# Decode attention with a channel MLP: w2's last rows as 68 rows with four zeroed copies, and x's rows spread over 64 partitions

## The chip, the cores and the metric

The kernel runs on one core of one Trainium2 chip. The metric is the device time of one execution in microseconds, the median of several runs. Everything on VectorE (DVE), ScalarE (ACT), GpSimd (POOL), TensorE (PE) and SyncE (SP) is ordered by semaphores that the kernel sets itself.

## The reference

One decode step for 8 sequences (B = 8, one token each, D = 640) with 32 heads of 128 and a cache of 4096 keys, plus an MLP with F = 1728, all in bf16:

```
xn  = layernorm(x)
q   = xn @ wq                                  # (8, 32 heads, 128)
p   = softmax(q k^T / sqrt(128))               # 4096 keys per head and sequence
att = (p v) @ wo
y   = layernorm(xn)
mlp = gelu(y @ w1 + b1) @ w2 + b2
out = x + att + mlp
```

The two caches are 268 MB each; all else together is under 16 MB.

## The kernel before

**Tiles.** The work goes in NQ = 32 items: item i is one sequence and a group of 8 heads. Its keys fill 128 partitions x 32768 elements, 64 KB in each partition: a k tile and a v tile of 8.4 MB. SBUF holds three such slots, `S_sb[:, 0..2]`: k tiles alternate between slots KA and KB, every v tile goes to slot VS. The slots also hold the small data while they are free: `wq_sb` lies in VS before v tile 0; `x_sb`, `xn_sb`, `y_sb` and the norm's numbers lie in KB before k tile 1; w1 and w2 come into KA after the last k tile there. `w2b_sb` (w2's last rows) and `ones_sb` have a place of their own.

**Order.** Nothing is scheduled by a planner. Each step is entered with `at(position, function)`, the steps are sorted by position, and each adds its instructions to the list of its engine; the lists are then replayed. Within an engine the order is that of the positions. `wait` puts a semaphore wait ahead of the next instruction of an engine, and everything behind it on that engine waits too.

**Start.** SP issues wq, k tile 0, then (after the q matmuls, `tk["qmm"]`) k tile 1 and v tile 0. ACT issues x, b2 and w2b. GpSimd makes iotas and constants (`consts_pool`). DVE makes the identity and masks (`idents`), then the layernorm (`norm(0)`, `norm(1)`); PE transposes the result (`pe_xT`), DVE copies it to `xT_sb` (`cp_xT`), PE starts the output accumulator with x and b2 (`pe_acc0`) and, once wq is there, makes q (`pe_q`), which DVE copies to `qT_sb` (`cp_q`).

**An item.** GpSimd writes the item's q into `qrep_sb` (`qrep`); PE and ACT turn it into `qbc_sb`, q on every partition (`pe_qbc`, `act_qbc`). DVE takes 176 of the 256 keys of a partition in three chunks: multiply by q, add halves, reduce (`dve_chunk`). The other 80 are transposed by PE, evicted by ACT (`act_T`) and multiplied by PE (`pe_QK`); DVE picks them (`dve_sel`), finds the maximum (`dve_max`), ACT makes the exponentials (`act_exp`), PE multiplies with v (`pe_PV`). GpSimd normalizes (`o_norm`). `k_ready` is a GpSimd memset of one column behind a wait for the k tile, which PE's transposes wait for. GpSimd's order begins with the constants, then qrep(0), k_ready(0), qrep(1), and so on.

**Releases.** SP issues k tile i when DVE and PE have finished tile i - 2 (`tk[("km", i - 2)]`, `tk[("kt", i - 2)]`), and v tile i when PE has finished v tile i - 1:

```
            if i >= 2:
                sp.wait(tk[("kt", i - 2)], tk[("km", i - 2)])
            elif s == KB:
                sp.wait(tk["qmm"])
```

**MLP.** F = 13 x 128 + 64: 13 blocks of 128 rows (FB) and a last one of FLAST = 64 rows, whose rows of w2 are `w2b_sb`. `pe_mlp1`, `act_gelu` and `pe_mlp2` run while the last item's k tile is being worked on.

Of the kernel before, what the change touches and what calls it, by code (L numbers as in the profile page):

```python
# [9 lines left out]
F32 = mybir.dt.float32  # L10
# [4 lines left out]
P = 128  # L15
# [177 lines left out]
def bass_parallel_sum__gqa_block_cached__mixer_channel_mlp__decode_kernel(  # L193
# [13 lines left out]
    B, _, D = A_x.shape  # L207
    _, H, SK, DH = A_k_cache.shape
    F = B_w1.shape[1]
# [5 lines left out]
    NQ = NHQ * B  # L215
    DC = D // P
    FB = F // P
    FLAST = F - FB * P
    SCALE = float(DH) ** -0.5
    TPB = 8  # L220
    NS = 2
# [5 lines left out]
    RW = P // HW  # L227
    NL = 3
    WN_CUT = (0, 5, 7, HS)
    V_CUT = (0, 192, 256)  # L230

    def jp_of(i):
# [14 lines left out]
    x2 = A_x.rearrange("b s d -> (b s) d")  # L247
    out2 = out.rearrange("b s (c n) -> (b s c) n", n=P)

    with ExitStack() as es:  # L250
# [7 lines left out]
        def part(slot, lo, n, rows=P):  # L258
            return S_sb[0:rows, slot, lo:lo + n]
# [3 lines left out]
        def scratch(n, rows=P, slot=KB):  # L263
            ap = part(slot, o_[slot], n, rows)
            o_[slot] += n + n % 2
            return ap
# [8 lines left out]
        woW_sb = part(KB, 0, HW * D)  # L275
        woL_sb = part(KB, HW * D, 2 * HS * D).rearrange("p (g x) -> p g x", g=2)
        b2_sb = scratch(D, 1)
        x_sb = scratch(D, B)
        xn_sb = scratch(D, B)
        y_sb = scratch(D, B)  # L280
        st_sb = scratch(64, B).bitcast(F32).rearrange("p (w n) -> p w n", w=2)
        iota_i = scratch(2 * P).bitcast(I32)
        iota_h = scratch(2 * HS).bitcast(I32)
        mtmp = scratch(2 * 2 * HS).bitcast(F32).rearrange("p (w n) -> p w n", w=2)
# [5 lines left out]
        ones_sb = sb("ones_sb", [1, B], BF)  # L290
        w2b_sb = sb("w2b_sb", [FLAST, D], BF)
        xT_sb = sb("xT_sb", [P, 2, DC, B], BF)
# [11 lines left out]
        ident_bf = sb("ident_bf", [P, P], BF)  # L304
# [16 lines left out]
        TR_ps = ps("TR_ps", [P, 2, TPB * P], BF)  # L321
# [4 lines left out]
        ACC_ps = ps("ACC_ps", [P, 512], F32)  # L326
# [8 lines left out]
        pe, dve, act, sp, pool = (_Eng(sem(f"{n}_s")) for n in ("pe", "dve", "act", "sp", "pool"))  # L335
        pe2, act2 = _Eng(sem("pe2_s")), _Eng(sem("act2_s"))
        ld_s = [_Dma(sem(f"ld_s{s}")) for s in range(3)]
        ld_x, ld_b1, ld_b2, ld_wq, ld_w1, ld_w2a, ld_w2b, st_o = (
            _Dma(sem(n)) for n in ("ld_x", "ld_b1", "ld_b2", "ld_wq", "ld_w1", "ld_w2a", "ld_w2b", "st_o"))
        ld_vl = [_Dma(sem(f"ld_vl{q}")) for q in range(1, len(V_CUT) - 1)]  # L340
        ld_wl = [_Dma(sem(f"ld_wl{q}")) for q in range(2)]
        ld_wn = [_Dma(sem(f"ld_wn{q}")) for q in range(len(WN_CUT) - 1)]
        tk = {}
        prog = []

        def at(pos, fn, *a):
            prog.append((pos, len(prog), fn, a))

        def load(key, dma, dst, src, eng=None):
            tk[key] = dma.sig((eng or sp).dma_start(dst, src))  # L350
# [18 lines left out]
        def load_v(i):  # L369
# [4 lines left out]
            tk[("v", i)] = []  # L374
            for d, lo, hi in zip([ld_s[VS]] + ld_vl, V_CUT[:-1], V_CUT[1:]):
                if lo:
# [15 lines left out]
        def load_wn(q):  # L392
            lo, hi = WN_CUT[q], WN_CUT[q + 1]
            n = HS * DH
            tk[("wn", q)] = ld_wn[q].sig(sp.dma_start(
                woL_sb[:, 1, lo * D:hi * D],
                A_wo[NL * n:(NL + 1) * n, :].rearrange("(p s) n -> p (s n)", p=P)[:, lo * D:hi * D]))

        def consts_pool():
            pool.iota(iota_h, [[-HP, HS]], base=0, channel_multiplier=1)  # L400
            pool.iota(iota_w, [[-RW, HW]], base=0, channel_multiplier=1)
            tk["iota"] = pool.sig(pool.iota(iota_i, [[1, P]], base=0, channel_multiplier=-1))
            for d, (ap, v) in zip([None] + ld_vl + [None] * 2, (
                    (zeros_sb, 0.0), (ones_sb[:, :], 1.0), (mx_sb[:, :], 0.0), (mb_sb[:, :], 0.0))):
                inst = pool.memset(ap, v)
                if d is not None:
                    inst.call[3] = (d.sem, 1)
            tk["consts"] = pool.sig(pool.memset(ones_f[:, :], 1.0))
# [45 lines left out]
        def pe_xT(w):  # L454
            src = xn_sb if w == 0 else y_sb
            pe.wait(tk["xn" if w == 0 else "y"], tk["id"])
            TRB[w].use(pe)
            for c in range(DC):
                last = pe.transpose(TR_ps[:, w, c * B:(c + 1) * B], src[:, c:D:DC], ident_bf[0:B, 0:B])
            TRB[w].used(pe, pe.sig(last))  # L460

        def cp_xT(w):
            TRB[w].use(dve)
            tk[("xT", w)] = TRB[w].used(dve, dve.sig(dve.tensor_copy(
                xT_sb[:, w, :, :].rearrange("p c b -> p (c b)"), TR_ps[:, w, 0:DC * B])))

        def pe_q():
            pe.wait(tk["wq"], tk[("xT", 0)])
# [12 lines left out]
        def pe_acc0():  # L481
            pe.wait(tk["consts"], tk["x"], tk["b2"], tk["id"])
            pe.matmul(ACC_ps[:, 0:DC * B], zeros_sb, zeros_sb[:, 0:DC * B], start=True, stop=False,
                      skip_group_check=True)
            for c in range(DC):
                pe.matmul(ACC_ps[:, c * B:(c + 1) * B], x_sb[:, c * P:(c + 1) * P], ident_bf[0:B, 0:B],
                          start=False, stop=False, skip_group_check=True)
                pe.matmul(ACC_ps[:, c * B:(c + 1) * B], b2_sb[:, c * P:(c + 1) * P], ones_sb[:, :],
                          start=False, stop=False, skip_group_check=True)

        def fcols(c):
            return (slice(c, FB * P, FB), P) if c < FB else (slice(FB * P, F), FLAST)

        def pe_mlp1():
            pe.wait(tk["w1"], tk["b1"], tk[("xT", 1)])
            TRB[1].use(pe)
            for c in range(FB + 1):
                cols, rows = fcols(c)
                o = HT_ps[0:rows, c * B:(c + 1) * B]
                for kc in range(DC):  # L500
                    pe.matmul(o, w1_sb[:, kc, cols], xT_sb[:, 1, kc, :], start=(kc == 0), stop=False)
                last = pe.matmul(o, b1_sb[:, cols], ones_sb[:, :], start=False, stop=True)
            TRB[1].used(pe, pe.sig(last))

        def act_gelu():
            TRB[1].use(act)
            act.activation(hT_sb[:, 0:FB, :].rearrange("p c b -> p (c b)"), HT_ps[:, 0:FB * B],
                           ACT.Gelu_apprx_tanh)
            tk["h"] = TRB[1].used(act, act.sig(act.activation(
                hT_sb[0:FLAST, FB, :], HT_ps[0:FLAST, FB * B:(FB + 1) * B], ACT.Gelu_apprx_tanh)))  # L510

        def pe_mlp2():
            pe.wait(tk["h"], tk["w2a"], tk["w2b"])
            for fc in range(FB + 1):
                rows = P if fc < FB else FLAST
                w = w2_sb[:, fc, :] if fc < FB else w2b_sb
                for c in range(DC):
                    last = pe.matmul(ACC_ps[:, c * B:(c + 1) * B], w[:, c * P:(c + 1) * P],
                                     hT_sb[0:rows, fc, :], start=False, stop=False, skip_group_check=True)
            tk["mlp"] = ACCB.used(pe, pe.sig(last))  # L520
# [132 lines left out]
        def pe_PV(i):  # L653
            PVB.use(pe)
            pe.wait(tk[("exp", i)])
            for j in range(NKEY):
                if j == 0:
                    pe.wait(tk[("v", i)][0])
                elif j in V_CUT:
                    pe.wait_ge(ld_vl[V_CUT.index(j) - 1].sem, 1)  # L660
                last = pe.matmul(PV_ps[:, 0:HS], tile[VS][:, j, :], P_sb[:, :, j],
# [89 lines left out]
        def fin_wn(q):  # L751
            lo, hi = WN_CUT[q], WN_CUT[q + 1]
            pe.wait(tk[("wn", q)], tk[("oS", 3, 0)], tk[("oS", 3, 1)])
            for r in range(lo, hi):
                for c in range(DC):
                    last = pe.matmul(ACC_ps[:, c * B:(c + 1) * B],
                                     woL_sb[:, 1, r * D + c * P:r * D + (c + 1) * P], oS3_sb[:, r, :],
                                     start=False, stop=(r == HS - 1), skip_group_check=True)
            if hi == HS:
                ACCB.used(pe, pe.sig(last))  # L760
# [12 lines left out]


        Q = 100.0
        at(-900, load, "x", ld_x, x_sb, x2, act)
        at(-898, load, "b2", ld_b2, b2_sb, B_b2.rearrange("(o f) -> o f", o=1), act)
        at(-890, load, "wq", ld_wq, wq_sb, A_wq.rearrange("(p c) n -> p c n", c=DC))
        at(NQ * Q - 55, load_mlp)
        at(-897, load, "w2b", ld_w2b, w2b_sb[:, :], B_w2[FB * P:F, :], act)  # L780
        at(-870, load_k, 0)
        at(-800, consts_pool)
        at(-795, idents)
        at(NQ * Q - 60, sel_pool)
        at(-790, norm, 0)
        at(-780, pe_xT, 0)
        at(-776, maskw)
        at(-775, cp_xT, 0)
# [7 lines left out]
        at(NQ * Q - 11.5, pe_mlp1)  # L796
        at(NQ * Q - 11, act_gelu)
        at(NQ * Q + 4.6, pe_mlp2)
        for i in range(NQ):
            o = i * Q  # L800
            last = i == NQ - 1
# [8 lines left out]
            w = 42.0 / nt  # L810
# [20 lines left out]
        o = NQ * Q  # L831
        for q in range(2):
            at(o + 50 + 0.1 * q, load_wl, q)
            at(o + 79.1 + 0.2 * q, fin_wl, q)
        for q in range(len(WN_CUT) - 1):
            at(o + 51 + q, load_wn, q)
# [71 lines left out]
```

## Time and profile before

| | before |
|---|---|
| median of 3 runs | 1282.38 us (1282.24 to 1282.55) |
| profiled execution | 1282.34 us |
| its span | 1281.0 us |
| DVE busy | 1103.0 us, 86% |
| PE busy | 672.2 us, 52% |
| ACT busy | 476.1 us, 37% |
| POOL busy | 100.0 us, 8% |
| bytes moved | 551.99 MB at 431 GB/s over the span |
| mean granted TensorE clock | 0.557 |

Times on the page are microseconds from the span's start. Nearly all instructions carry line 111, the line that replays the lists, so groups are told apart by the names out<-in. A line of the timeline gives start, duration, engine, operation with shape, and in brackets the idle time before it and what ended that. "SPq" and "ACTq" lines are DMA issues of SP and ACT. q1 is SP's DMA queue, q10 is ACT's; each runs on the core's 16 DMA engines. Packet records, one for each packet with its queue, start, duration and size, are part of the trace; where a text says "packet records", numbers come from these.

### The profile page before, as it was taken

What the parts mean: (1) busy time and instruction counts of PE and PEld (TensorE: products, weight loads), DVE (VectorE), ACT (ScalarE), POOL (GpSimd) and SP (SyncE); (2) the same over time, 40 slices, a digit from 0 to 9 for tenths busy, and PEclk for the clock granted to TensorE, in tenths of its full rate; (3) what the DMA queues carried; (4) which work ended last, traced back from release to release, by engine and by line L of the source; (5) the groups of instructions that cost most, each with busy time, mean ns of one, the idle gap of its engine ahead of it and who ended that gap; (6) DMA issues with size and microseconds to landing.
All of it is one profiled execution on the core that took longest, in us unless ns stands there. A gap on an engine that the chain in (4) does not pass through costs nothing.

```text
span 1281.0 us, 34439 instructions
## 1 busy us (share of the span) xinstructions
PE 672.2 (52%) x13944; PEld 575.5 (45%) x13944; DVE 1103.0 (86%) x680; ACT 476.1 (37%) x905; POOL 100.0 (8%) x110
## 2 busy tenths in 40 slices
PE   1546555446545446555456554456454466464476
PEld 1435445345534345444345444345343355353365
DVE  1899999889888899888898888898888898888895
ACT  0524444233444233443234443234443234442331
POOL 0000010000000000000000000000000000000040
PEclk9755565555555555555565565555555565555565
DMA  9999999999999999999999999999999999999998
GB/s 400 445 422 436 432 432 434 434 436 432 432 432 440 428 432 436 440 426 432 438 438 428 430 436 442 428 430 436 440 430 428 436 436 436 426 438 432 432 439 361
DMA packets 10675, 551.99 MB, mean 431 GB/s; under 512 B 1244, under 2 KB 1445, under 8 KB 1702
## 3 DMA queue, kind: packets, MB, share of 16 engines
q1 hardware_dynamic: 10512, 551.70, 99.7%
q8 instruction: 9, 0.15, 0.0%
q10 hardware_dynamic: 150, 0.11, 0.0%
q14 instruction: 4, 0.03, 0.0%
HBM read 551.80 MB, written 0.01 MB: 431 GB/s over the span
## 4 chain that ended last, share of the span: by engine, by line
DMA 52%; DVE 36%; issue 11%; DVEq 0%; PE 0%; SPq 0%; ACT 0%
DMA S_sb<-in_A_k_cache_dram 51%; DVE S_sb L111 26%; DVE Sd_sb L111 8%; DMA S_sb<-in_A_wo_dram 2%; DVE S_ps L111 1%; DVE ri_sb L111 0%; DVEq L109 0%; PE ACC_ps L111 0%; DVE mx_sb L111 0%; SPq L111 0%; DVE mbT_sb L111 0%; DVE mxT_sb L111 0%; DVE mq_sb L111 0%; DVE mb_sb L111 0%; PE QB_ps L111 0%
## 5 line engine op out<-in xcount | busy, mean ns | idle before, releaser
L111 PE MATMUL TR_ps<-ident_bf,S_sb 128*128 128x128 bf16 (+1 forms) x2570 | 342.9, 280 | 353.5 <-POOL kr_sb L111 341.6
L111 DVE TENSOR_TENSOR S_sb<-S_sb,qbc_sb 128x7552 bf16<-128x7552 bf16 (+1 forms) x96 | 392.6, 4089 | 128.4 <-DMA S_sb<-in_A_k_cache_dram 128.1
L111 PEld LDWEIGHTS TR_ps<-ident_bf,S_sb 128*128 (+2 forms) x2570 | 245.4, 103 | 411.6 <-issue 337.7
L111 DVE TENSOR_REDUCE Sd_sb<-S_sb 128x59 f32<-128x3776 bf16 (+1 forms) x96 | 390.2, 4064 | 6.0
L111 ACT ACTIVATE KT_sb<-TR_ps 128x1024 bf16<-128x1024 bf16 x320 | 326.5, 1023 | 122.0 <-PE TR_ps L111 110.9
L111 PE MATMUL PV_ps<-P_sb,S_sb 128*128 128x8 bf16 x8192 | 224.0, 175 | 137.4 <-DMA S_sb<-in_A_v_cache_dram 134.5
L111 PEld LDWEIGHTS PV_ps<-P_sb,S_sb 128*128 128x128 bf16 x8192 | 221.5, 103 | 140.1 <-DMA S_sb<-in_A_v_cache_dram 137.3
L111 DVE TENSOR_TENSOR S_sb<-S_sb 128x3776 bf16<-128x3776 bf16 (+1 forms) x96 | 204.6, 2131 | 3.3
L111 ACT ACTIVATE P_sb<-Sd_sb,NB_sb 128x256 bf16<-128x256 f32 x256 | 126.3, 494 | 213.4 <-DVE NB_sb L111 213.4
L111 PE MATMUL S_ps<-qrep_sb,KT_sb 128*128 128x8 bf16 x2560 | 121.9, 177 | 51.6 <-ACT KT_sb L111 48.4
L111 ACT ACTIVATE oU_sb<-PV_ps 128x8 f32<-128x8 f32 x31 | 5.5, 177 | 375.6 <-PE PV_ps L111 375.6
L111 PEld LDWEIGHTS S_ps<-qrep_sb,KT_sb 128*128 128x128 bf16 x2560 | 91.8, 103 | 83.0 <-ACT KT_sb L111 42.1
L111 POOL TENSOR_TENSOR oT_sb<-oU_sb,ri_sb 128x8 bf16<-128x8 f32 x31 | 71.8, 2315 | 378.8 <-DVE S_sb L111 303.2
L111 POOL COPY qrep_sb<-qT_sb 128x128 bf16<-128x128 bf16 x32 | 14.5, 453 | 475.3 <-PE S_ps L111 455.2
L111 ACT ACTIVATION_READ_ACCUMULATOR P_sb<-Sd_sb,NB_sb 128x1 f32 x256 | 47.8, 187 | 0.0
L111 DVE TENSOR_TENSOR S_ps<-S_ps,mask_sb 128x320 f32<-128x320 f32 (+1 forms) x65 | 31.6, 486 | 2.6 <-PE S_ps L111 2.6
L111 DVE TENSOR_REDUCE Sd_sb<-S_ps 128x40 f32<-128x320 f32 x64 | 31.5, 491 | 2.2
L111 PE MATMUL QB_ps<-ident_bf,qrep_sb 128*128 128x128 bf16 x32 | 9.1, 284 | 41.2 <-DVE S_sb L111 21.4
L111 ACT ACTIVATE qbc_sb<-QB_ps 128x128 bf16<-128x128 f32 x32 | 8.9, 277 | 58.0 <-PE QB_ps L111 58.0
L111 POOL MEMSET kr_sb<- 128x1 f32 x32 | 3.1, 98 | 294.7 <-DMA S_sb<-in_A_k_cache_dram 294.7
L111 PEld LDWEIGHTS QB_ps<-ident_bf,qrep_sb 128*128 128x128 bf16 x32 | 3.3, 103 | 44.1 <-ACT oU_sb L111 29.5
L111 PE MATMUL CH_ps<-rs_sb,ones_f 128*128 128x8 f32 x64 | 16.5, 330 | 6.6 <-ACT P_sb L111 6.6
(71 smaller groups left out, 147.0 us busy)
## 6 DMA issues: line engine op xcount, KB each, us to landing
S_sb<-in_A_v_cache_dram SPq DMA_DIRECT2D x1, 6144.0 KB, 26.8
S_sb<-in_A_wq_dram SPq DMA_DIRECT2D x1, 5120.0 KB, 16.0
S_sb<-in_A_wo_dram SPq DMA_DIRECT2D x1, 2560.0 KB, 16.5
S_sb<-in_B_w_dram SPq DMA_DIRECT2D x1, 2160.0 KB, 30.3
S_sb<-in_B_w_dram SPq DMA_DIRECT2D x1, 2080.0 KB, 34.8
S_sb<-in_A_v_cache_dram SPq DMA_DIRECT2D x1, 2048.0 KB, 31.3
S_sb<-in_A_wo_dram SPq DMA_DIRECT2D x1, 1280.0 KB, 19.3
S_sb<-in_A_wo_dram SPq DMA_DIRECT2D x1, 800.0 KB, 20.8
```

The source lines that it names most:

```text
L111: inst = getattr(e, name)(*a, **k)
```

## The change

Two parts. First, w2's last block becomes FLAST = 68 rows: the last 64 rows of F and the four before them, which block structure also computes in the 13 full blocks. The four doubled rows of `w2b_sb` are set to zero by GpSimd after the load (`zero_w2b`), and `pe_mlp2` waits for that. The new step stands in GpSimd's order behind the constants and ahead of qrep(0). As 68 rows the load runs on four DMA engines; as 64 it ran on 16.

Second, x's eight rows go to partitions 0, 8, ..., 56 of a 64-partition `x_sb`, which GpSimd sets to zero first (`zero_x`, ahead of its constants); ACT's x load waits for that (`load_x`). The layernorms run on 64 partitions, the transposes give 64 columns of which `cp_xT` takes every eighth, and `pe_acc0` takes every eighth column of the identity.

```diff
-    FLAST = F - FB * P
+    FREST = F - FB * P
+    FLAST = FREST + 4
...
+    XP = 8 * B
...
-        x_sb = scratch(D, B)
-        xn_sb = scratch(D, B)
-        y_sb = scratch(D, B)
-        st_sb = scratch(64, B).bitcast(F32).rearrange("p (w n) -> p w n", w=2)
+        x_sb = scratch(D, XP)
+        xn_sb = scratch(D, XP)
+        y_sb = scratch(D, XP)
+        st_sb = scratch(64, XP).bitcast(F32).rearrange("p (w n) -> p w n", w=2)
...
+        def zero_x():
+            tk["xz"] = pool.sig(pool.memset(x_sb, 0.0))
+
+        def load_x():
+            act.wait(tk["xz"])
+            load("x", ld_x, x_sb[0:XP:8, :], x2, act)
...
-                last = pe.transpose(TR_ps[:, w, c * B:(c + 1) * B], src[:, c:D:DC], ident_bf[0:B, 0:B])
+                last = pe.transpose(TR_ps[:, w, c * XP:(c + 1) * XP], src[:, c:D:DC],
+                                    ident_bf[0:XP, 0:XP])
...
-                xT_sb[:, w, :, :].rearrange("p c b -> p (c b)"), TR_ps[:, w, 0:DC * B])))
+                xT_sb[:, w, :, :], TR_ps[:, w, 0:DC * XP].rearrange("p (c b o) -> p c b o", c=DC, o=8)[:, :, :, 0])))
...
-                pe.matmul(ACC_ps[:, c * B:(c + 1) * B], x_sb[:, c * P:(c + 1) * P], ident_bf[0:B, 0:B],
+                pe.matmul(ACC_ps[:, c * B:(c + 1) * B], x_sb[:, c * P:(c + 1) * P], ident_bf[0:XP, 0:XP:8],
...
-            return (slice(c, FB * P, FB), P) if c < FB else (slice(FB * P, F), FLAST)
+            return (slice(c, FB * P, FB), P) if c < FB else (slice(F - FLAST, F), FLAST)
...
+        def zero_w2b():
+            pool.wait(tk["w2b"])
+            tk["w2z"] = pool.sig(pool.memset(w2b_sb[0:FLAST - FREST, :], 0.0))
...
-            pe.wait(tk["h"], tk["w2a"], tk["w2b"])
+            pe.wait(tk["h"], tk["w2a"], tk["w2z"])
...
-        at(-900, load, "x", ld_x, x_sb, x2, act)
+        at(-905, zero_x)
+        at(-900, load_x)
...
-        at(-897, load, "w2b", ld_w2b, w2b_sb[:, :], B_w2[FB * P:F, :], act)
+        at(-897, load, "w2b", ld_w2b, w2b_sb[:, :], B_w2[F - FLAST:F, :], act)
...
         at(-800, consts_pool)
+        at(-799, zero_w2b)
         at(-795, idents)
```

## The prediction

> **What bounds the kernel now.** I read the page's slices and queues first. The profiled execution took 1282.34 us: a span of 1281.0 and 1.34 around it. The median of the three runs, 1282.38, is the same within 0.04, so what I add to the span I add to the median.
>
> ```profile
> DMA  9999999999999999999999999999999999999998
> q1 hardware_dynamic: 10512, 551.70, 99.7%
> q10 hardware_dynamic: 150, 0.11, 0.0%
> ```
>
> q1 is SP's queue (k, v and the big weights), q10 is ACT's (x, b2, w2b, b1, out). The 16 DMA engines are full from start to end on q1, so every microsecond in which SP has nothing queued moves the end, and compute costs only where it starves the queue. By the packet records no engine stands empty between 2 us and the tail. So the question is which buffer release comes too late. The timeline of the first 75 us has the releases:
>
> ```profile
> 0.74 0.60 ACTq L111 DMA_DIRECT2D S_sb<-in_A_x_dram  x1
> ...
> 1.63 0.53 ACTq L111 DMA_DIRECT2D w2b_sb<-in_B_w_dram  x1
> ...
> 16.82 4.43 PE L111 MATMUL CH_ps<-xT_sb,S_sb 128*128 128x8 bf16 x160 [8.00 <-DMA S_sb<-in_A_wq_dram]
> ...
> 21.77 0.29 POOL L111 COPY qrep_sb<-qT_sb 128x128 bf16<-128x128 bf16 x1 [20.06 <-DVE qT_sb L111]
> ...
> 22.44 0.28 ACT L111 ACTIVATE qbc_sb<-QB_ps 128x128 bf16<-128x128 f32 x1 [15.19 <-PE QB_ps L111]
> 36.46 4.03 DVE L111 TENSOR_TENSOR S_sb<-S_sb,qbc_sb 128x7424 bf16<-128x7424 bf16 x1 [14.75 <-DMA S_sb<-in_A_k_cache_dram]
> ```
>
> The query copy for tile 0 (qrep, GpSimd) is done at 22.06, the broadcast at 22.72; VectorE then sits until k tile 0 lands. That 13.7 us of slack belongs to GpSimd's step. SP's own timeline gives what hangs on VectorE:
>
> ```profile
> 21.64 0.43 SPq L111 DMA_DIRECT2D S_sb<-in_A_v_cache_dram  x1
> 69.25 0.33 SPq L111 DMA_DIRECT2D S_sb<-in_A_k_cache_dram  x1
> 85.34 0.33 SPq L111 DMA_DIRECT2D S_sb<-in_A_v_cache_dram  x1
> 103.58 0.33 SPq L111 DMA_DIRECT2D S_sb<-in_A_k_cache_dram  x1
> 128.85 0.33 SPq L111 DMA_DIRECT2D S_sb<-in_A_v_cache_dram  x1
> ```
>
> These are v0, k2, v1, k3, v2. k2 is issued when VectorE has finished tile 0 (69.25 = 36.46 + 32.79). The engines finish v0 at 73.05 to 74.90 (packet records). An issue takes 1.0 us to its first packet (wq: issued 0.74, first packets 1.77), so k2 comes 4.65 us before the last engine runs dry. That is the margin I test the change against: **VectorE may start tile 0 at most 4.65 us later, by 41.1.**
>
> **The change, part by part.**
>
> *x.* A GpSimd memset of 64x640 bf16 now precedes ACT's x load. Rows: 128x128 bf16 0.20 us, 128x128 f32 0.24; by bytes (256 B 0.20, 512 B 0.24, here 1280 B) 0.36, by elements five times 0.20, 1.0. The load leaves at 1.1 to 1.8 instead of 0.74. Queued behind it on ACT's queue are b2 and w2b; on GpSimd the iotas. More matters that x now arrives after wq's packets. Before, x's rows were first on eight engines and landed by 3.0; b2, issued at 1.37, had its one row served at 5.8, after two wq packets. I put x's rows there too, its completion one wq packet (1.57) later, and x on VectorE at 7.5 to 9 instead of 3.03. From 3.03 to PE's last ACC_ps matmul at 8.8 is 5.8 us, so all of it ends by 15, ahead of 16.8 when wq lets PE start. Were it not hidden, q would be late against the 13.7 us of slack. Norms on 64 partitions cost VectorE the same (its width, 640, stays), transposes 64 columns wide instead of 8 some tens of ns. Sum: 0, and nothing beyond 16.8 would show it.
>
> *w2b.* Before: 64 rows over 16 engines, four each, 14.3 us to land. How ACT's rows share an engine with SP's is in the DMA counts of the stretch 6.8 to 8.3 us:
>
> ```profile
> q1 hardware_dynamic: 15, 0.61, 96.9%
> q10 hardware_dynamic: 15, 0.02, 3.2%
> ```
>
> One small packet for one big one: a 1280 B row, 55 ns itself, waits out a 40 KB packet of wq, 1.51 to 1.65 us. The packet records say the same of one engine: b2's row at 5.8, b2's completion at 7.35, then four w2b rows, the completion at 15.4, each one wq packet after the one before; a 4-byte completion takes a turn of its own. On four engines each gets 17 rows, and the turns now last longer, since k tile 0 follows wq with 64 KB packets of 2.42 us.
>
> Count on the first engine: x row, x completion, b2 row, b2 completion, 17 rows, completion = 22 turns of q10, the n-th after q1's item n+1. Item 23 of q1: 8 wq packets and a completion, 8 of k0 and a completion, then the fifth packet of k1. k0 starts there at 15.4; 13 x (2.42 + 0.06) = 32.2, so w2b completes at 47.6, on GpSimd 0.5 later (k0: last completion 35.99, VectorE 36.46).
>
> By the Trainium skill, DMA: Bandwidth & Descriptors, section "Why a DMA increments its semaphore by 16 and not by 1", the engines are the largest number up to 16 that divides both sides' slowest dimension, which gives 4 for 68 rows. The trace agrees for 64 rows (16 completions) and x's 8 (8); no run here shows 68. Without that rule I have the title's "four", and the rows' ends: 16 engines (five rows each, landed near 17.5, cost 0) and one (b2: all 73 turns, done when v0 drains at 75, VectorE 40 late).
>
> *zero_w2b.* The new memset waits for w2b, and behind it in GpSimd's order stand qrep(0), k_ready(0) and all the rest; PE waits for qrep(0) with tile 0's transposes, ACT with the broadcast, VectorE with its first product. Price: 48.1, memset of 4x640 0.36 to 1.0 (0.5 taken, close to the byte rule), and 0.95 from qrep's start to the broadcast's end: VectorE starts at 49.6. **D = 49.6 - 36.46 = 13.2 us.** Less 4.65 of margin: the engines run dry from 74.9 until 69.25 + 13.2 + 1.0 = 83.5, **8.6 us**.
>
> *What is late next.* v2 waits for PE's tile 1, which hangs on ACT's exp(1) after VectorE's tile 1: 128.85 + 13.2 + 1.0 = 143.05, while k3, 133.16 before, now ends at 133.16 + 8.6 = 141.76: another **1.3 us**. v1 and k3 keep a margin: k3's issue 103.58 + 13.2 = 116.8 against v1's end 113.8 + 8.6 = 122.4. Later VectorE needs 34.5 us for a tile against 38.7 for the two transfers, gains 4.2 a tile and opens no further gap. The tail follows the transfers.
>
> *The last block with 68 rows* (PE, Gelu): same instruction counts, PE reads 68 weight columns instead of 64; 0, under 0.1 us. It sits before the last v lands.
>
> Sum: 8.6 + 1.3 = 9.9. The restart itself could add 0.5: wq's first packets took 1.9 to 2.7 us against 1.51. **1282.38 + 9.9 = 1292.3.**
>
> **The rivals.**
>
> *Nothing is starved (not slower).* An engine takes several q10 rows in one turn. Place: engines 0 to 3 between 5 and 47 us; it decides if w2b completes before 39.1 (41.1 less 0.5, 0.5 and 0.95), that is if the 22 turns shrink to 18. With all rows in one or two turns w2b lands before 15, GpSimd's memset ends long before 21.77, and what is left is x's rows no longer ahead of wq: the engine that began wq last, at 2.67, begins near 1.8. Time 1281.5 to 1282.4. For it: nothing here shows turns against 64 KB packets. Against it: 1:1 in the counts above, for four turns running on every engine. The Trainium skill, the same page, section "Queues, rings and completion order", says an engine drains a whole packet, typically 9 to 17 descriptors, from one ring before it switches; by that this rival would hold, and the trace's one row a turn speaks against it. Chance 0.07.
>
> *The 68 rows don't go to four engines* but to 16, as the 64 did: landed near 17.5, no cost, 1282.4. Chance 0.03; one or two engines (some 36 us more), 0.02.
>
> *Turns counted wrong.* If x still gets ahead of wq, or some completions take no turn, w2b is one or two turns of 2.48 earlier: D 10.7 or 8.2, time 1289.8 or 1287.3 (total D - 3.3). If q1's completions take no turn, two later: D 18.2, 1297.3. Same mechanism, other size. Chance 0.13 earlier, 0.07 later.
>
> *Faster.* Only x's place in the queue (0.9 us) and four rows fewer on 12 engines (0.23) gain: 1281.2 at best, no difference that can be measured. Chance of more 0.03, for a stagger of the engines (1.3 to 1.9 us in each landing) that I may misread.
>
> **How the numbers follow.** My count 0.65, the rest as above. About 0.2%, 2.6 us, can be told from no change. The low end, 1285, takes in the two turns fewer and a bubble shorter than counted; the high end, 1297, one turn more, the restart and a slow memset. Outside are the two uncosted cases (0.10), the faster one (0.03) and part of the later ones. Slower 0.65 + 0.13 + 0.07 + 0.02 = 0.87; same 0.10; faster 0.03.
>
> **What would show it.** w2b's issue to landing near 46 us instead of 14.3. GpSimd idle until 48, its reason w2b, then qrep. VectorE's first 128x7424 product at 49.6, k2's issue at 82.5, engines empty from 74.9 to 83.5, v2's issue near 142. x lands at 7.5 to 9, PE still starts on wq at 16.8. The forecast is wrong if w2b lands before 39, or if k2 is issued before 74 all the same.

## The result and the profile after

The changed kernel takes 1295.5 us, median of 5 runs (1295.26 to 1298.42), against 1282.38 us: 13.1 us more. The ratio on record is 1.0106 (95% interval 1.0092 to 1.0121; the two medians alone give 1.0102). The forecast was 1292.3 in a range of 1285.0 to 1297.0. The profiled execution took 1296.06 us with a span of 1294.7, 13.7 us longer than before's.

The profile's slices and queues, as shown of before:

```profile
DMA  9969999999999999999999999999999999999998
q1 hardware_dynamic: 10512, 551.70, 98.8%
q10 hardware_dynamic: 142, 0.11, 0.0%
```

The same bytes, but the third slice (64.7 to 97.1 us) is no longer full. The timeline of the first 52 us, the lines that answer to those of before:

```profile
1.39 1.16 ACTq L111 DMA_DIRECT2D S_sb<-in_A_x_dram  x1
...
2.90 0.26 ACTq L111 DMA_DIRECT2D w2b_sb<-in_B_w_dram  x1
...
9.21 0.88 DVE L111 BATCH_NORM_STATS2 S_sb<-S_sb 64x6 f32<-64x320 bf16 x2 [6.49 <-DMA S_sb<-in_A_x_dram]
...
16.17 4.43 PE L111 MATMUL CH_ps<-xT_sb,S_sb 128*128 128x8 bf16 x160
20.64 0.42 DVE L111 CAST qT_sb<-CH_ps 128x256 bf16<-128x256 f32 x1 [5.64 <-PE CH_ps L111]
...
48.67 0.63 POOL L111 MEMSET w2b_sb<- 4x640 bf16 x1 [46.39 <-DMA w2b_sb<-in_B_w_dram]
49.24 0.28 POOL L111 COPY qrep_sb<-qT_sb 128x128 bf16<-128x128 bf16 x1
...
49.90 0.28 ACT L111 ACTIVATE qbc_sb<-QB_ps 128x128 bf16<-128x128 f32 x1 [36.32 <-PE QB_ps L111]
50.29 4.02 DVE L111 TENSOR_TENSOR S_sb<-S_sb,qbc_sb 128x7424 bf16<-128x7424 bf16 x1 [29.23 <-ACT qbc_sb L111]
```

q is ready at 21.06, 0.6 us earlier than before, but GpSimd, idle for 46.39 us, waits for w2b until 48.67. VectorE's first product, which before waited for k tile 0, now waits for the broadcast of q and starts 13.83 us later. SP's timeline gives what hangs on it:

```profile
21.00 0.43 SPq L111 DMA_DIRECT2D S_sb<-in_A_v_cache_dram  x1
83.08 0.33 SPq L111 DMA_DIRECT2D S_sb<-in_A_k_cache_dram  x1
99.17 0.33 SPq L111 DMA_DIRECT2D S_sb<-in_A_v_cache_dram  x1
117.31 0.33 SPq L111 DMA_DIRECT2D S_sb<-in_A_k_cache_dram  x1
142.63 0.33 SPq L111 DMA_DIRECT2D S_sb<-in_A_v_cache_dram  x1
```

k2 is issued 13.83 us later than before and v2 13.78. The windows view of the stretch around it, after (columns: stretch, its length, busy us of PE, PEld, DVE, ACT and POOL with instruction counts, granted clock, DMA share, GB/s):

```profile
73.00:76.00 3.00, 2.98 (x45) 2.46 (x44) 3.00 (x1) 2.37 (x3) 0.00 (x0) 0.50 0.00 0
76.00:84.00 8.00, 6.50 (x87) 4.91 (x85) 7.79 (x7) 5.83 (x6) 0.29 (x1) 0.50 0.01 3
84.00:88.00 4.00, 0.00 (x0) 0.00 (x0) 3.93 (x4) 3.33 (x13) 0.00 (x0) 0.50 1.37 524
...
142.00:148.00 6.00, 3.02 (x40) 2.26 (x36) 5.93 (x3) 0.46 (x2) 2.65 (x2) 0.50 0.98 350
148.00:240.00 92.00, 51.16 (x986) 42.98 (x985) 87.66 (x52) 43.30 (x82) 5.82 (x7) 0.56 1.00 433
```

(A packet counts in the stretch in which it starts.) From 75.0, where the last engine ends v0, to 84.0 no big packet starts. A second, partial gap shows at 143: 350 GB/s instead of the 433 of the stretch beyond. The packet records put the last engine's completions behind those of before by 0.1 us at v0, 11.5 at k2 (105.80 against 94.28), 11.3 at v1 and at k3, 13.9 at v2 (166.41 against 152.50), and 13.7 to 13.9 from there to the end. All of the loss is made before 167 us, in two places.

### The profile page after: what moved, and what is told of

It is laid out like the page before. It is cut to its first block, busy times and chain, and to the rows that moved or that the text cites. A ratio compares the mean times of both kernels' runs of the same rounds, so it can differ in the third digit from the quotient of the medians.

```text
span 1294.7 us, 34441 instructions
## 1 busy us (share of the span) xinstructions
PE 673.5 (52%) x13944; PEld 576.7 (45%) x13944; DVE 1102.9 (85%) x680; ACT 476.8 (37%) x905; POOL 101.2 (8%) x112
## 4 chain that ended last, share of the span: by engine, by line
DMA 52%; DVE 35%; issue 11%; PE 1%; DVEq 0%; POOL 0%; SPq 0%; ACT 0%; ACTq 0%; POOLq 0%
DMA S_sb<-in_A_k_cache_dram 44%; DVE S_sb L111 26%; DVE Sd_sb L111 7%; DMA w2b_sb<-in_B_w_dram 4%; DMA S_sb<-in_B_w_dram 2%; DMA S_sb<-in_A_wo_dram 2%; DVE S_ps L111 1%; PE TR_ps L111 1%; DVEq L109 0%; DVE ri_sb L111 0%; PE ACC_ps L111 0%; DVE mx_sb L111 0%; POOL S_sb L111 0%; PE QB_ps L111 0%; PE S_ps L111 0%
## 5 line engine op out<-in xcount | busy, mean ns | idle before, releaser
L111 POOL COPY qrep_sb<-qT_sb 128x128 bf16<-128x128 bf16 x32 | 14.8, 462 | 462.0 <-PE S_ps L111 462.0
## 6 DMA issues: line engine op xcount, KB each, us to landing
S_sb<-in_A_wo_dram SPq DMA_DIRECT2D x1, 2560.0 KB, 16.5
S_sb<-in_B_w_dram SPq DMA_DIRECT2D x1, 2080.0 KB, 34.8
```

Source lines behind the costliest of these rows:

```text
L111: inst = getattr(e, name)(*a, **k)
```

## Experiments: the wait or the load

Four variants take the change apart. The theory: w2b's 17 rows on each of four engines take turns with SP's big packets, complete at 48 us, and hold up qrep(0). Rival 1: x's part costs. Rival 2: the load costs by itself.

**The w2 part alone.**

```diff
 at(-800, consts_pool)
+at(-799, zero_w2b)
...                      # x as in the kernel before, w2b as in the change
```

> Only the w2 part (68 rows, four doubled rows zeroed before the first qrep); x is loaded as before, ahead of wq. Theory (each of ACT's rows and completions takes one turn against one big packet of SP's queue): without x's two turns behind wq the first engine has 20 turns instead of 22, w2b completes after the third packet of k tile 1, near 42.7 us instead of 48.2, GpSimd's memset at 43.2, VectorE's first product at 44.8 (D 8.4 instead of 13.8), and the time is about 5 us shorter than the whole change: 1290 to 1291. Rival 1 (x's part is what costs, through a late q): 1282.4. Rival 2 (the load costs by its engine time on four engines, wherever the wait stands): as the whole change, 1295.5.

Measured: 1290.57 us (1290.2 to 1291.96), ratio 1.0062 (1.0045 to 1.0079). Three lines of its timeline, GpSimd's memset and SP's issues of k2 and v2:

```profile
44.53 0.62 POOL L111 MEMSET w2b_sb<- 4x640 bf16 x1 [42.82 <-DMA w2b_sb<-in_B_w_dram]
...
78.94 0.33 SPq L111 DMA_DIRECT2D S_sb<-in_A_k_cache_dram  x1
...
138.22 0.33 SPq L111 DMA_DIRECT2D S_sb<-in_A_v_cache_dram  x1
```

Without x's two turns w2b is zeroed 4.14 us earlier and the time is 4.9 us shorter. The memset came 1.3 us later than I had put it: the packet records have the 20 turns as counted, but the last completion at 44.03 instead of 42.7, and why was not followed up. The step in time is as expected. Rival 1 falls; x's part matters only by the two turns that it puts in front of w2b.

**x's part alone.** `FLAST = FREST`, no `zero_w2b`.

> Only x's part (GpSimd zeroes 64 partitions first, x's rows on every eighth partition); w2's last block has 64 rows over 16 engines as before. Theory: x lands near 9 us and PE still starts on wq at 16 to 17, w2b lands two or three turns later than before, near 20, and nobody waits for it: 1282.0 to 1282.8. Rival 1 (x is what costs): 1288 or more.

Measured: 1282.62 us (1282.36 to 1282.97), ratio 1.0001 (0.9992 to 1.0011). w2b takes 15.7 us from issue to landing instead of 14.3, and VectorE starts tile 0 at 36.49 (36.46 before). Free, as expected.

**The wait moved, the load kept.**

```diff
-at(-799, zero_w2b)
+at(NQ * Q - 59, zero_w2b)
```

> The whole change, but GpSimd waits for w2b and zeroes its doubled rows behind the selections for the last items, some 1200 us later. The load itself is the same: 68 rows on four engines, completed near 48 us. Theory (the wait ahead of qrep(0) is all of the cost): k tile 2 issued near 69 us, time 1282 to 1283. Rival 2 (the load's place on four engines costs by itself): 1286 to 1296. Half and half: 1288.

Measured: 1282.77 us (1282.41 to 1283.52), ratio 1.0003 (0.9993 to 1.0012). The load is the same, its last completion at 48.48 us by the packet records, but GpSimd does not stand in front of it:

```profile
21.35 0.29 POOL L111 COPY qrep_sb<-qT_sb 128x128 bf16<-128x128 bf16 x1 [19.08 <-DVE qT_sb L111]
```

VectorE starts at 36.42, k2 goes out at 69.20. So the four-engine load by itself costs nothing that can be told from no change, and with the wait moved away from qrep(0) the whole 13 us is gone. Rival 2 falls.

**The wait kept, the load on 16 engines.**

```diff
-FLAST = FREST + 4
+FLAST = FREST + 16
```

> The whole change with 80 rows instead of 68 (16 doubled rows, zeroed); more rows, but the load goes over 16 engines with five rows each, and GpSimd's wait stands where the change has it. Theory: w2b completes about three or four turns later than before, 20 to 24 us, GpSimd's memset and qrep(0) are done by 26, VectorE starts at 36.4 when k tile 0 lands: 1282 to 1283. Rival (any wait for w2b at this place costs): 1290 or more. If 80 rows don't spread over 16 engines: 1295 or more.

Measured: 1282.58 us (1282.35 to 1282.69), ratio 1.0001 (0.9991 to 1.0010). More rows, zeroed at the same place, and no cost that can be told:

```profile
21.05 0.62 POOL L111 MEMSET w2b_sb<- 16x640 bf16 x1 [18.77 <-DMA w2b_sb<-in_B_w_dram]
22.05 0.29 POOL L111 COPY qrep_sb<-qT_sb 128x128 bf16<-128x128 bf16 x1 [0.38 <-DVE qT_sb L111]
```

80 rows spread over 16 engines and are zeroed by 21.67, just ahead of q. The wait is harmless if the load is quick: both are needed for the loss.

## Experiments: turns, queue, and what lateness costs

**Two turns more.** `FLAST = FREST + 12`: 76 rows, 19 on each of four engines.

> The whole change with 76 rows (12 doubled rows, zeroed): four engines with 19 rows each, two turns more on each. Theory: w2b completes two packets of 2.4 to 2.5 us later, near 53 us, VectorE starts near 55.2 (D 18.7), and the time grows by those 5 us: 1300 to 1301. If the cost has another cause than the turns (a fixed price of the wait, or of having four engines): 1295 to 1296, as with 68 rows.

Measured: 1301.27 us (1300.7 to 1301.6), ratio 1.0146 (1.0129 to 1.0163), 5.8 us above the 68 rows. GpSimd's line:

```profile
53.84 0.63 POOL L111 MEMSET w2b_sb<- 12x640 bf16 x1 [51.57 <-DMA w2b_sb<-in_B_w_dram]
```

5.17 us later than with 68 rows: two turns of 2.59. The time follows the turns; a fixed price falls.

**The same load on SP's queue.**

```diff
-at(-897, load, "w2b", ..., act)
+at(-885, load, "w2b", ...)          # SP, behind wq, ahead of k tile 0
```

> The whole change, but SP issues w2b's 68 rows, behind wq and ahead of k tile 0, instead of ACT. Still four engines and 17 rows each, and GpSimd's wait stays ahead of qrep(0). Theory: in SP's own queue the 17 rows follow wq without taking turns (17 x 0.055 = 0.9 us of four engines), w2b lands by 17 to 18 us, before q is ready at 21: 1282 to 1283.5. Rival (four engines cost by themselves): 1290 or more.

Measured: 1282.42 us (1282.3 to 1282.65), ratio 1.0000 (0.9990 to 1.0009).

```profile
16.77 0.63 POOL L111 MEMSET w2b_sb<- 4x640 bf16 x1 [14.49 <-DMA w2b_sb<-in_B_w_dram]
```

Four engines, 17 rows each, landed by 16.8 instead of 48.7. The 80 rows before also sat in the second queue, with five on each engine, and were quick. What makes the load slow is the two together: 17 rows on one engine, in a second queue beside one that always has a big packet ready.

**Lateness without any load.** GpSimd waits for k tile 0 and then runs n memsets of 128x2048 ahead of qrep(0), in the kernel before:

```diff
+def hold():
+    pool.wait(tk[("k", 0)])
+    for _ in range(n):
+        pool.wait(pool.sig(pool.memset(KT_sb[:, :, :, :], 0.0)))
 at(-800, consts_pool)
+at(-799, hold)
```

> The same with seven such memsets, about 13.3 us: VectorE starts 14 us late with no change to any load. Theory (the late start of tile 0 is all that costs): k tile 2 issued near 83.3 us, the engines without work from 75 to 84, another late v tile 2 near 143, and a time as the whole change's, 1295 to 1297. Rival (part of the change's 13 us comes from the loads): 1288 to 1293.

n = 7 measured: 1296.92 us (1295.41 to 1297.48), ratio 1.0114 (1.0097 to 1.0130). VectorE starts at 50.71, 14.25 us late, k2 goes out at 83.50. With the loads of the kernel before, the late start alone gives a loss as large as the change's (14.5 us for 14.25 us of lateness, beside 13.1 for 13.83).

> The kernel before, with GpSimd waiting for k tile 0 and then one memset of 128x2048 bf16 (about 1.9 us by the rate of the 64x640 one) ahead of qrep(0); nothing else changes. Theory: VectorE starts about 2.9 us late, within the 4.65 us that the queue has in hand, k tile 2 issued near 72.2 us, and the time stays at 1282.4 (within 0.4). Rival (VectorE's start is itself on the path): 1285 or more.

n = 1 measured: 1285.37 us (1284.67 to 1285.89), ratio 1.0023 (1.0013 to 1.0033). Here my expectation was wrong: VectorE starts 2.95 us late (39.41), inside the 4.65 us that I had called free, and 3.0 us are lost. SP's timeline shows where:

```profile
72.21 0.33 SPq L111 DMA_DIRECT2D S_sb<-in_A_k_cache_dram  x1
...
131.50 0.33 SPq L111 DMA_DIRECT2D S_sb<-in_A_v_cache_dram  x1
```

and the windows view of that kernel around v2 (columns as above):

```profile
128.00:131.00 3.00, 3.00 (x119) 3.00 (x117) 2.93 (x7) 0.00 (x0) 0.00 (x0) 0.50 0.96 415
131.00:135.00 4.00, 0.75 (x19) 0.47 (x15) 3.97 (x2) 0.46 (x2) 2.94 (x2) 0.50 0.90 328
```

k2's transfer ends 0.74 us behind before's (last completion 95.02 against 94.28); v2's ends 2.59 behind (155.09 against 152.50). So I formed a second theory: v2 is the tighter place, and tested it with two more.

> As the run with one memset, but GpSimd only waits for k tile 0 ahead of qrep(0): VectorE starts about 1.0 us late. Theory A (the tight place is v tile 2, which before is issued 128.85 us and starts 1.3 us ahead of the first engine's end of k tile 3 at 131.1; with one memset it is issued at 131.5 and the last engine loses 1.65 us): v2 issued near 129.9, nothing runs dry, 1282.4 to 1283.0. Theory B (any lateness of tile 0 is passed on, about 1 us for 1 us): 1283.4.

n = 0 measured: 1283.16 us (1282.37 to 1284.15), ratio 1.0005 (0.9996 to 1.0014). The interval takes in no change, though nine of the eleven runs lie above the slowest of the 16 of before (1282.64). VectorE is 0.97 us late:

```profile
70.22 0.33 SPq L111 DMA_DIRECT2D S_sb<-in_A_k_cache_dram  x1
...
129.44 0.33 SPq L111 DMA_DIRECT2D S_sb<-in_A_v_cache_dram  x1
```

In the profiled run v2's last completion is 1.07 us behind, and k2's is not behind at all (0.03 us ahead). Theory A had nothing run dry. The packet records show two engines that stood empty all the same, until they began v2 at 131.76 and 132.32, and the first of these packets took 4.04 us. So there is less in hand at v2 than the 1.3 us of theory A, and theory B's 1283.4 lies as near.

> As the run with one memset, with two: VectorE starts about 4.7 us late, k tile 2 issued near 74.0, its first packets near 75.0. The prediction's margin of 4.65 us would have made this free. Theory A (two tight places: v2 with 1.3 us in hand, k2 with 2.9 for the first engine and 4.7 for the last): a short gap at k2 and a longer one at v2, 4 to 5 us in all, 1286.5 to 1287.5. If k2 alone counted: 1282.4 to 1283.5.

n = 2 measured: 1287.12 us (1285.66 to 1288.15), ratio 1.0035 (1.0022 to 1.0048).

```profile
74.10 0.33 SPq L111 DMA_DIRECT2D S_sb<-in_A_k_cache_dram  x1
...
133.63 0.33 SPq L111 DMA_DIRECT2D S_sb<-in_A_v_cache_dram  x1
```

VectorE is 4.85 us late, k2's last completion 2.36 us behind, v2's 4.96. Both places count, and a margin at k2 alone falls. The time is in theory A's range, but one for one (1287.2) would give it too, so these runs do not tell a small margin at v2 from none. All runs side by side (lateness of VectorE's first product and of v2's last completion, from the profiled runs):

| kernel | VectorE late, us | v2 late, us | time over before, us |
|---|---|---|---|
| hold, n = 0 | 0.97 | 1.07 | 0.8 |
| hold, n = 1 | 2.95 | 2.59 | 3.0 |
| hold, n = 2 | 4.85 | 4.96 | 4.7 |
| w2 part alone | 9.69 | 9.63 | 8.1 |
| the change | 13.83 | 13.91 | 13.1 |
| hold, n = 7 | 14.25 | 13.26 | 14.5 |
| 76 rows | 19.01 | 18.73 | 18.9 |

The times are medians. Of the w2 part alone the profiled run was the longest (1291.96, 9.6 over before's), of the hold with n = 7 the shortest (1295.41, 13.1 over), so where a row's last two columns differ, the profiled run's own time follows v2. The lateness of the first product is passed on nearly one for one from the first microsecond or so.

## Why the prediction was right, and where its sum was off

**Turns: right.** w2b's last completion came at 48.16 us by the packet records (47.6 counted), with 22 turns on the first engine and 20 on the three others, which completed at 42.5 to 42.6. The DMA counts of the stretch 16.5 to 33 us, after, show one row for one packet against 64 KB packets too:

```profile
q1 hardware_dynamic: 111, 7.27, 102.8%
q10 hardware_dynamic: 28, 0.04, 0.6%
```

A quarter of 111 is 27.75 packets for the four engines, beside 28 of q10. That rules out the rival that had several rows served in a turn. The Trainium skill, DMA: Bandwidth & Descriptors, section "Queues, rings and completion order", has an engine drain a whole packet, typically 9 to 17 descriptors, before it switches. This trace does not agree: each turn of q10 took one row of 1280 B. The completions of wq and k0 took turns as counted: two rows pass together on each engine at 14.8 to 15.3 and at 34.8 to 35.4.

**Four engines: right.** 68 rows of w2 went with four completions. By the Trainium skill, the same page, section "Why a DMA increments its semaphore by 16 and not by 1", 80 rows take 16 engines and 76 take four. The runs agree: 16 completions, the last at 20.5, and four, the last at 53.3.

**The wait and what is behind it: right.** VectorE at 50.29 (49.6 forecast), k2 at 83.08 (82.5), v2 at 142.63 (142.05). D was 13.83 instead of 13.2: 0.56 for the later completion, and 0.57 for the memset up to qrep instead of 0.5. (49.6 - 36.46 is 13.14, so the forecast's own D is 13.1; the slip is under 0.1 us.)

**x: right in cost, thin in cover.** x came at 9.21, a little beyond the 7.5 to 9, and the chain from there took 6.87 us instead of 5.8. It ended at 16.08 rather than 15, 0.1 us ahead of the q matmuls. A little more would have delayed q; w2b would still have hidden that, and x's part alone is free.

**The sum: too small.** Two terms failed.

The margin: "VectorE may start tile 0 at most 4.65 us later" looked at k2 and at the last engine only. v2 stood in my own sum as the next late thing, but not as a margin of its own. Before, it is issued at 128.85 and the first engine ends k3 at 131.08. With 1.0 us from issue to first packet that leaves 1.2 us in hand, not 4.65. Even 1.2 is too much, because 1.0 is only the shortest of these delays. By the packet records, engines that stood empty began v2 1.06 to 3.16 us after its issue in the change, and 0.95 to 3.23 us after it in the hold with n = 1. With n = 0 v2 is issued 1.57 us ahead of the first engine's end of k3, and two engines still stand empty, until 2.32 and 2.88 us after the issue. The hold with n = 1 lost 3.0 us inside the margin. The bound that I gave for the rival on the other side, w2b complete by 39.1, was therefore at least 3 us too late. For the change itself the place did not matter, since it is far beyond both.

The restart: taken at 0, with 0.5 allowed in the range from wq's first packets, of which twelve took 1.9 to 2.7 us and the other four 1.51 to 1.63. The last engine was 11.5 us behind at k2, of which 8.6 was forecast and 0.6 is D. k2's first packets took 2.98 to 3.32 us on nearly all engines, 0.6 to 0.9 over the steady 2.42. The remaining 1.6 or so is that the engines, which began k2 within 1.1 us of each other, ended it spread over 1.8 again, while I had let the last one gain its whole lag from the new start. In other words, 8.6 was the gap of the engine that ended v0 last, at 75.0; the first had ended at 73.3, and on average the 16 stood empty about 10.0 us (packet records, 60 to 100 us, less before's). v2 added 2.4 to 2.6 us where 1.3 was forecast; its first packets took up to 3.9, and one began only at 145.79, though v2 was issued at 142.63 and no engine worked on k3 after 144.49. Why first packets are slow and why one engine begins so late is not settled by these runs.

## What to carry to other kernels

In these runs a small load on a second queue beside a saturated one cost one big packet per row, 2.4 to 2.6 us each at 64 KB. Its landing time is then about (rows on its busiest engine + what is queued ahead) times the big packet, and a wait on it belongs behind everything that the saturated stream needs. Choose row counts that spread over all engines (80 rows landed by 21 us, 68 by 48.7), or put the small load into the busy queue itself (16.8). For a full queue, take the margin at every release in the first items, against the first engine that runs dry, not the last, and with the longest delay from issue to first packet, not the shortest (here over 3 us and 1.0).

## What the runs showed of the hardware that was not expected

A queue that has run dry does not resume at full pace: first packets of 64 KB took 3.0 to 3.3 us at k2 and up to 3.9 at v2, against 2.42; between 200 and 1200 us only two of some 6600 such packets took over 2.6. An engine need not stand empty for it. In the kernel before, v2 is issued 2.2 us ahead of the first engine's end of k3, no engine stands empty, and the first two packets of v2 took 2.88 and 3.42 us. So it may be the late issue that counts and not the empty engine; no run here separates the two.

With one memset held ahead of qrep(0), the last engine was 0.92 us behind before's at the end of k3 and 2.59 at the end of v2: 1.7 us lost for 0.54 us of idle time per engine (mean of 16 between 120 and 140 us, packet records). It was not won back: the span is 2.5 us longer, 1283.5. Nor do the other engines take up what one has lost. In the change the engines were 12.7 us behind before's on average at the end of v2 and the last one 13.9; near 1200 us they were 12.5 and 13.7 behind, and the time follows the last.
